# V weights in five pieces from ScalarE's queue, x blocks first in SyncE's queue, and a newly found order of the whole program

## The chip, the core and the metric

The kernel runs on one core of one Trainium2 chip. The metric is the device time of one execution in microseconds (us). Before the change it is 1747.95 us, the median of three runs (1744.44 to 1748.0).

## What is computed

Four layers one after the other over a sequence of 2048 rows of 512: memory-augmented attention A, a gated feed-forward block B, then A and B again with the same weights. Cut to what matters:

```python
def _A_ref(x, mem0, Wq, Wk, Wv, Wo, seg_len):      # H = 32 heads of 128, M = 8, seg_len = 32
    mem = mem0
    for s in range(S // seg_len):                  # 64 segments, one after the other
        h = concatenate([mem, x[:, s*seg_len:(s+1)*seg_len]], axis=1)      # 8 + 32 rows
        q, k, v = h @ Wq, h @ Wk, h @ Wv           # each 512 -> 32 heads x 128
        p = softmax(where(mask, q @ k.T * scale, -1e9))
        o = (p @ v) @ Wo
        mem = o[:, :8]                             # carried to the next segment
        outs.append(o[:, 8:])
def _B_ref(x, w_gate, w_up, w_down):
    return (sigmoid(x @ w_gate) * (x @ w_up)) @ w_down
x = x + _A_ref(layernorm(x), ...); x = x + _B_ref(layernorm(x), ...)       # twice
```

The carried memory makes the 64 segments of one attention layer a chain.

## The kernel before, in words

Both attention layers run interleaved: step t handles segment t of the first and segment t - 6 of the second (`emit_step`). A feed-forward block follows every four steps (`ffn`, 128 rows at a time, its weights streamed again each time from HBM by POOL's DMA queue). The weights of q, k, v and o (4 MB each) lie in SBUF for the whole run.

The stretch that this document is mostly about is the **boot**, up to the end of step 0:

- **Loads.** `load_weights` (L359) issues the weights from SyncE (SP): V in eight pieces of four heads (0.5 MB each, L370 to L374), each from the third on behind a wait for an earlier piece (`after`, L373, realised at L1233), with the x blocks that the boot needs put between them two at a time (L377). Then q and k in pieces of 3, 6 and 7 heads (384, 896 and 768 columns) and Wo in pieces of three heads. All DMAs of SP take one of eight semaphores in turn, so a DMA also waits until the DMA eight places before it has landed.
- **V in advance.** For most rows of the first layer V does not depend on the memory. `v_group` normalises an x block on VectorE (L582 to L586), transposes it on TensorE (L595), copies it to `xvf` on ScalarE or VectorE (L1228, L1230), and `v_pass` multiplies it with `wv_sb` (L635): eight groups of four matmuls of 512 columns per 128 rows, each group with its own 512 columns (four heads) of V. The results go through SBUF to a scratch tensor in DRAM (`scr`) and from there to `vsb`. Rows that do not fill a tile go through narrower strips of 64 columns (L673) and 32 columns (L762).
- **Step 0.** q and k (L868), scores (L904), softmax, transposed probabilities (L950), times V (L976), times Wo (L995). The first q and k matmuls can start as soon as their pieces of weights and the transposed x block 0 are there.
- **Fillers.** Where the plan sees TensorE without work for more than a quarter of a microsecond, it puts matmuls on a tile of zeros, `hot` (L1214), there to keep the clock up. At the start of the program this is a run of 23.

What comes when is not decided by the order of the Python lines. Each operation becomes a task of a planner (`Planner`). `SEQUENCE`, a packed string, holds the place of every task in one global order and, for tasks that two engines can do, the engine. `replay` walks this order with the planner's constants (durations, DMA rates, latencies), hands out buffers and computes where fillers go and what POOL's large weight loads are paced by. Each engine then runs its tasks in that order, and the waits between engines are derived from the data.

Of the kernel before, what the change touches and what calls it, by code (L numbers as in the profile page):

```python
# [1293 lines left out]
```

## Time and profile before

| | |
|---|---|
| median of three runs | 1747.95 us (1744.44, 1747.95, 1748.0) |
| span of the profiled execution, first to last instruction | 1747.1 us |
| TensorE (PE) busy | 1733.4 us, 99% |
| VectorE (DVE) busy | 1248.4 us, 71% |
| ScalarE (ACT) busy | 1128.5 us, 65% |
| GpSimd (POOL) busy | 859.0 us, 49% |
| moved by DMA | 273.41 MB, 156 GB/s over the span |
| granted TensorE clock | 1.000 |

Only the span of the profiled execution is known, not a time of its own; it lies between the lowest and the highest of the three runs. PE's busy time counts a matmul from its start to a modelled end, so that back-to-back matmuls leave no idle time; PEld is the loading of weights into the array, beside it. SP has no busy time: it only issues DMAs, and its rows (SPq) show when an issue began and how long it took. A releaser after an arrow is who ended the idle time before an instruction.

### The profile page before, as it was taken

The page shows a single profiled execution, that of the slowest core. Times are in us where ns is not written, and L with a number is a line of the kernel's source. Part 1 is how long each engine was busy: PE and PEld are TensorE (multiplying, and loading weights), DVE is VectorE, ACT ScalarE, POOL GpSimd, SP SyncE. Part 2 cuts the span into 40 slices and gives each one's busy share as a digit, 9 for nine tenths or more (in the row PEclk, how much of TensorE's full clock was granted, in tenths as well). Part 3 has the DMA queues.
Part 4 walks back from the last instruction along what each step waited for, and adds up shares of the span by engine and source line. Part 5 has one row for each costly group of instructions (what it writes and reads, how often), then busy time and mean ns, then how long its engine had stood idle before and what let it go on. Part 6 is the DMA issues. An engine that isn't in the chain of part 4 may idle for free.

```text
span 1747.1 us, 91842 instructions
## 1 busy us (share of the span) xinstructions
PE 1733.4 (99%) x39162; PEld 1491.8 (85%) x39162; DVE 1248.4 (71%) x4208; ACT 1128.5 (65%) x3119; POOL 859.0 (49%) x1367
## 2 busy tenths in 40 slices
PE   9999999999999999999999999999999999999998
PEld 4688789889898988989888888989888888988886
DVE  5677777677767776786777767776777776767676
ACT  3576777566666766666666666666665666666564
POOL 5624345635544554445445554544455364454543
PEclk9999999999999999999999999999999999999999
DMA  8935355645645555545555464545455464554644
GB/s 285 320 100 155 109 151 161 195 113 153 174 130 163 156 159 143 165 125 164 152 148 158 136 184 128 166 138 153 132 174 166 139 174 128 144 156 131 178 120 134
DMA packets 145583, 273.41 MB, mean 156 GB/s; under 512 B 39686, under 2 KB 86018, under 8 KB 145174
## 3 DMA queue, kind: packets, MB, share of 16 engines
q0 software_dynamic: 72944, 198.79, 39.8%
q1 hardware_dynamic: 72230, 68.75, 13.3%
q8 instruction: 307, 5.03, 1.2%
q14 instruction: 102, 0.84, 0.2%
HBM read 221.78 MB, written 27.07 MB: 142 GB/s over the span
## 4 chain that ended last, share of the span: by engine, by line
PE 94%; DMA 3%; DVE 1%; SPq 1%; issue 1%; POOL 0%; ACT 0%; POOLq 0%; ACTq 0%
PE bank L868 34%; PE bank L995 17%; PE bank L1097 12%; PE bank L762 8%; PE bank L635 6%; PE bank L1120 6%; PE bank L904 4%; PE bank L976 4%; PE bank L950 2%; PE bank L595 1%; PE bank L1214 1%; DMA wk_sb<-in_A_Wk_dram 1%; DMA wo_sb<-in_A_Wo_dram 0%; PE bank L1065 0%; DMA scr<-wu 0%
## 5 line engine op out<-in xcount | busy, mean ns | idle before, releaser
L868 PE MATMUL bank<-hT,wq_sb 128*128 128x80 bf16 (+3 forms) x8960 | 616.4, 198 | 1.0 <-DVE hT L1008 0.3
L868 PE MATMUL bank<-hT,wk_sb 128*128 128x80 bf16 (+3 forms) x8960 | 616.3, 198 | 0.8 <-DMA wk_sb<-in_A_Wk_dram 0.6
L1228 ACT CAST qku<-bank 128x480 bf16<-128x480 f32 (+4 forms) x770 | 384.7, 508 | 223.7 <-PE bank L868 194.6
L868 PEld LDWEIGHTS <-wq_sb 128*128 128x128 bf16 x8960 | 454.2, 99 | 32.1 <-issue 15.1
L868 PEld LDWEIGHTS <-wk_sb 128*128 128x128 bf16 x8960 | 446.9, 99 | 1.1 <-DMA wk_sb<-in_A_Wk_dram 0.7
L995 PE MATMUL bank<-otsb,wo_sb 128*128 128x80 bf16 (+1 forms) x8960 | 360.2, 198 | 2.2 <-DMA wo_sb<-in_A_Wo_dram 1.3
L918 DVE TENSOR_TENSOR st<-bank,cst 40x240 f32<-40x240 f32 (+3 forms) x768 | 280.5, 368 | 113.2 <-PE bank L904 97.5
L995 PEld LDWEIGHTS <-wo_sb 128*128 128x128 bf16 x8960 | 336.6, 99 | 15.5 <-DMA wo_sb<-in_A_Wo_dram 2.0
L1228 ACT CAST otsb<-bank 128x480 bf16<-128x480 f32 (+3 forms) x420 | 200.2, 483 | 83.4 <-PE bank L976 52.8
L1090 POOL DMA_DIRECT2D wu<-in_B_w_up_dram x217 | 166.5, 768 | 170.0 <-PE bank L950 36.4
L1114 POOL DMA_DIRECT2D wd<-in_B_w_down_dram x217 | 156.9, 723 | 182.0 <-PE bank L1120 39.6
L1224 POOL DMA_DIRECT2D vsb<-sst x351 | 178.2, 512 | 129.6 <-ACT sst L1228 64.7
L1089 POOL DMA_DIRECT2D wg<-in_B_w_gate_dram x217 | 166.4, 767 | 138.1 <-PE bank L1097 56.7
L928 ACT ACTIVATE st<-st 80x240 f32<-80x240 f32 (+3 forms) x420 | 159.2, 381 | 58.0 <-DVE st L925 54.8
L1097 PE MATMUL bank<-xnT,wg 128*128 128x128 bf16 (+2 forms) x1784 | 171.5, 218 | 0.0
L1097 PE MATMUL bank<-xnT,wu 128*128 128x128 bf16 (+2 forms) x1784 | 171.1, 218 | 0.0
L930 DVE TENSOR_REDUCE small<-st 80x6 f32<-80x240 f32 (+3 forms) x420 | 151.5, 363 | 23.4 <-ACT st L928 20.2
L1220 ACT ACTIVATE ptsb<-bank,small 120x160 bf16<-120x160 bf16 (+3 forms) x430 | 156.6, 386 | 17.2 <-PE bank L950 10.7
L904 PE MATMUL bank<-qku 128*128 128x80 bf16 (+1 forms) x2240 | 162.7, 197 | 1.0 <-issue 0.9
L925 DVE TENSOR_TENSOR st<-st,small 80x240 f32<-80x240 f32 (+3 forms) x420 | 155.0, 370 | 5.7
L939 DVE TENSOR_TENSOR pb<-st,small 80x240 bf16<-80x240 f32 (+3 forms) x420 | 154.1, 370 | 5.7
L923 DVE TENSOR_REDUCE small<-st 80x6 f32<-80x240 f32 (+3 forms) x420 | 152.5, 364 | 6.2
(108 smaller groups left out, 2554.1 us busy)
## 6 DMA issues: line engine op xcount, KB each, us to landing
wg<-in_B_w_gate_dram POOLq DMA_DIRECT2D x220, 256.0 KB, 4.2
wu<-in_B_w_up_dram POOLq DMA_DIRECT2D x220, 256.0 KB, 4.2
wd<-in_B_w_down_dram POOLq DMA_DIRECT2D x220, 256.0 KB, 3.9
vsb<-scr SPq DMA_DIRECT2D x137, 66.0 KB
scr<-vst SPq DMA_DIRECT2D x90, 96.0 KB
vsb<-scr POOLq DMA_DIRECT2D x93, 66.0 KB, 3.4
vsb<-sst SPq DMA_DIRECT2D x179, 32.0 KB
vsb<-sst POOLq DMA_DIRECT2D x169, 32.0 KB, 2.8
```

What stands on the lines that cost most here:

```text
L868: nc.tensor.matmul(o_ap, lhsT=W[:, c, h * P:(h + 1) * P], rhs=mv(c), start=(c == 0), stop=(c == DC - 1))
L904: nc.tensor.matmul(s_all(SB)[:, w0 + i, :], lhsT=fview(qku[:, i, 0, 0:1], [(1, P)]), rhs=qku[:, i, 1, 0:ncol], start=True, stop=True)
L918: pl.add("DVE", dve_ns(n, True), lambda gsz=gsz, hs=hs, st=st, SB=SB, pj_=pj_, npj_=npj_, mk=mk, idx=idx: nc.vector.tensor_tensor(out=st[p ...
L928: pl.add("ACT", act_ns(n), lambda hs=hs, st=st: nc.scalar.activation(out=st[pr, hs], in_=st[pr, hs], func=ACTF.Exp, scale=self.scale), r=s ...
L995: nc.tensor.matmul(WB[:, c * ncol:(c + 1) * ncol], lhsT=self.wo[:, h, c * P:(c + 1) * P], rhs=otsb[:, hl, 0:ncol], start=(h == 0 and c == ...
L1089: pl.add("POOL", 760, lambda wg=wg, fs=fs: nc.gpsimd.dma_start(out=wg[:], in_=self.wgv[:, :, fs]), r=[("wo", self.H - 1)], w=[gk] + bt, la ...
L1090: pl.add("POOL", 760, lambda wu=wu, fs=fs: nc.gpsimd.dma_start(out=wu[:], in_=self.wuv[:, :, fs]), r=[("wo", self.H - 1)], w=[uk] + bt, la ...
L1097: nc.tensor.matmul(gu[:, 2 * i + k, 0:n], lhsT=W[:, c, i * P:(i + 1) * P], rhs=xnT[:, c, rw], start=(c == 0), stop=(c == DC - 1))
L1114: pl.add("POOL", 760, lambda wd=wd, ip=ip: nc.gpsimd.dma_start(out=wd[:], in_=self.wdv[:, 2 * ip:2 * ip + 2, :]), w=[dk] + (["boot"] if se ...
L1220: nc.scalar.activation(out=dst, in_=src, func=ACTF.Copy, scale=by)
L1224: {"SP": nc.sync, "POOL": nc.gpsimd}[tk.on].dma_start(out=got[1], in_=got[2])
L1228: nc.scalar.copy(out=dst, in_=src)
```

## The change

V's weights come in five pieces (two of 4 heads, three of 8 heads) instead of eight. A piece may be issued by SP or by ACT; in the new order all five are on ACT. The waits of one piece for another (`after`) are gone. The x blocks are put between the pieces three at a time in the list of tasks, and in the new order they lead SP's queue. In the planner, `replay` now keeps a queue of transfers each for SP, ACT and POOL, with new constants, counts ACT's table load, and lets the semaphores' turn of eight cover ACT's DMAs too. `SEQUENCE` is replaced: the order of the whole program, on all engines, is another one.

Cut to the parts that the text speaks of:

```diff
-    BUS, BUS0, SLOW, BIG, ROOM, TAIL = 345.0, 290.0, 18000.0, 300000, 1.0, 1200.0
-    LEAD = {"SP": 1000.0, "POOL": 1800.0}
-    FIRST = {"PE": 0.0, "ACT": 2040.0, "DVE": 980.0, "POOL": 3500.0, "SP": 750.0}
+    BUS, BUS0, SLOW, BIG, ROOM, TAIL = 335.0, 304.0, 20400.0, 300000, 1.0, 1850.0
+    TAILP, CP, STEAL, FIX = 1000.0, 142.0, 0.4, 12400.0
+    LEAD = {"SP": 600.0, "ACT": 600.0, "POOL": 2800.0}
+    FIRST = {"PE": 0.0, "ACT": 800.0, "DVE": 980.0, "POOL": 3500.0, "SP": 750.0}
+    TABLE = 1240.0
...
-        bus = wbus = 0.0
+        bus, wbus = {"SP": 0.0, "ACT": 0.0, "POOL": 0.0}, 0.0
...
+            if (e == "SP" or e == "ACT" and tk.nb) and len(lanes) >= 8:
+                t = max(t, lanes[-8])
...
+            if e == "ACT" and not tk.nb and not table:
+                table, t = True, max(t, free[e] + self.TABLE)
...
-        def ld(dst, src, nb, keys, after=()):
-            return pl.add("SP", 480, lambda: nc.sync.dma_start(out=dst, in_=src), r=after, w=keys, boost=self.boot(), lat=1750.0, nb=nb)
+        def ld(dst, src, nb, keys, after=(), engs=("SP",)):
+            return pl.add(engs, {e: 480 for e in engs}, lambda: ("dma", dst, src), r=after, w=keys, boost=self.boot(), lat=1750.0, nb=nb)
 
         xb = list(self.boot_x)[1:]
-        for h0, n in ((0, 4), (4, 4), (8, 4), (12, 4), (16, 4), (20, 4), (24, 4), (28, 4)):
+        for h0, n in ((0, 4), (4, 4), (8, 8), (16, 8), (24, 8)):
             cs = slice(h0 * P, (h0 + n) * P)
-            tk = ld(self.wv[:, :, cs], wv_v[:, :, cs], P * self.DC * n * P * 2, [("wv", h) for h in range(h0, h0 + n)], [("wv", h0 - 8)] if h0 > 4 else [])
-            if h0 > 4:
-                tk.after = pl.writer[("wv", h0 - 8)]
+            ld(self.wv[:, :, cs], wv_v[:, :, cs], P * self.DC * n * P * 2, [("wv", h) for h in range(h0, h0 + n)], (), ("SP", "ACT"))
             if h0 == 0:
                 continue
-            for b in xb[:2]:
+            for b in xb[:3]:
                 self.load_x(b, *self.boot_x[b])
-            xb = xb[2:]
+            xb = xb[3:]
...
-                    {"SP": nc.sync, "POOL": nc.gpsimd}[tk.on].dma_start(out=got[1], in_=got[2])
+                    {"SP": nc.sync, "ACT": nc.scalar, "POOL": nc.gpsimd}[tk.on].dma_start(out=got[1], in_=got[2])
```

What the built programs' orders say of the boot, as instructions and without times:

- ACT's list begins: V heads 8 to 15 (1 MB); V heads 0 to 3, which waits for the semaphore of heads 8 to 15; V heads 4 to 7, which waits for that of the fourth x block; the table load; the copy into `xvf` that the first V group needs; V heads 16 to 23, waiting for the semaphore of a later x block; two copies; V heads 24 to 31, waiting for that of a small piece of Wo. Of the four later pieces each waits for a semaphore because it is the ninth or a later DMA in the turn of eight.
- SP's list begins with seven x blocks without a wait, then four more x blocks (three of the boot and block 1), each waiting for an earlier one, then the memory rows, a piece of Wo, the mask, and the q and k pieces.
- The first V group works on heads 8 to 11 (before: heads 0 to 3). The run of fillers at the start has 18 matmuls (17 of 512 columns and one of 384) instead of 23 (22 and one).
- Before the first q and k matmuls stand 22 V groups (before: 28), and the 64-column strips come after them, no longer ahead. Before the first matmul of step 1 there are 48 V groups and all of step 0 in both orders. The group of fillers between step 0 and step 1 is gone; two groups of 1280 columns each stand within step 0. Behind step 1's begin both orders hold nearly as many filler columns (11648 and 11776).

More of the change, by code (lines that the diff above doesn't have):

```diff
@@ new lines @@
+Ozvhl{wNq&Z&=^Qwg0xG0I{`(WWfk0i;>jDnf>k!)w-*;tC^*Gr{Nk-Jk3$19f=%hL5-5fXHxHV5&H#3q2kh^pB^)AueZdi~_o69owJ$zVTJgO=>FasOQ5XsL#N`p=tGvU9~86fs#sNiVT?EtZ^@z`=SB&cop<(@?_Nju`{73CCD%5
+45RNy#NQ^S1j!ah7e{Umg@8Ai{46i4eazo%+8kO=u@+igZ@AsDcjPyYaObY9wkN&!nvWWO<YyBtm<PbHfVa<`aLaZ5mbnBmj4M6XK6CI(eHooE-ti5DKN+nhN~1bY6H27+TC0k!-)_PlnAqQA*VN3Byce$s3D@L4UfTBb4Mu_jkq$u
+g6F`(yU~z9s>guSnT%Oo#|p^4&`ihU^E430QcM_4NY9Du#-&VbKQbK2I{9qCMM&zENc3cr>+$4{+Z)GGH&fHZ22j)i^v8&;BGI!r;RUCLWXZ6S#6sj-k(SvCK%v95!z}pS&N9rJLF>cW)Eob?8ZO=DaDIJ}j<MkcEH=ba!DupjdOqI
@@ L145 @@
+rFjzBBlr?Z9Fc4IlI3C_GnUQ~smjd)a(}7yYldAT4Lk?xnFl5xhT?fZ%jdy0`L!NpBzWwbunVnHb86tuRRE6$U|^kUsoMZ$do;LsKxm&hc%!Yc4f61*>bkP@7*LINHX#__gef@=EF%ebpeykkosL1+n_ms$=gU&A!qBmKAIpaE@aPB
+(Dr=NE+Nh;^K|l#q@kdQCkxNw-`@ZIBg%((*-Lm2U2C8SiUS++y4XLW3000
 """
@@ L276, in replay @@
         reads = {}
-        bus = wbus = 0.0
+        bus, wbus = {"SP": 0.0, "ACT": 0.0, "POOL": 0.0}, 0.0
         lanes, pes = [], []
+        table = False
         def ready(d, tk, gap):
@@ L320, in replay @@
             if tk.nb:
-                bus = max(bus, t + self.LEAD[e])
-                bus += tk.nb / (self.BUS0 if bus < self.SLOW else self.BUS)
-                tk.done = max(bus + self.TAIL, end + tk.lat + tk.slow * min(max(wbus - t, 0.0), self.BACK))
+                a = t + self.LEAD[e]
+                w = (tk.nb + self.FIX) / (self.BUS0 if t < self.SLOW else self.BUS)
+                late = min(max(wbus - t, 0.0), self.BACK)
+                if e == "POOL":
+                    busy = [q for q in ("SP", "ACT") if bus[q] > a]
+                    for q in busy:
+                        bus[q] += self.STEAL * w / len(busy)
+                    if busy:
+                        w = (tk.nb + self.FIX) / self.CP
+                else:
+                    q = "ACT" if e == "SP" else "SP"
+                    d = min(w, max(bus[q] - a, 0.0))
+                    bus[q] += d
+                    w += d
+                bus[e] = max(bus[e], a) + w
+                landed = bus[e] + (self.TAILP if e == "POOL" else self.TAIL)
+                tk.done = max(landed, end + tk.lat + tk.slow * late)
                 if e == "POOL" and tk.nb >= self.BIG:
                     wbus = max(wbus, t + self.LEAD[e]) + tk.nb / self.BUS
-            if e == "SP":
+            if e == "SP" or e == "ACT" and tk.nb:
                 lanes.append(tk.done)
-                if len(lanes) >= 8:
-                    free[e] = max(end, lanes[-8])
         self.span = max(free.values())
@@ L360, in waits @@
         for d in [T[i] for i in list(tk.deps) + tk.prev]:
-            k = d.on if d.on != "SP" else ("SP", d.tick)
+            k = d.on if d.on != "SP" and not (d.on == "ACT" and d.nb) else (d.on, "dma", d.tick)
             if d.tick > seen.get(k, 0):
```

175 lines of the change are left out of this document (83 added, 92 removed).

## The prediction

> **What bounds the kernel now.** I read the page first, for which engine is full. It shows the span, the busy times and the shares of the chain that ended last:
>
> ```profile
> span 1747.1 us, 91842 instructions
> PE 1733.4 (99%) x39162; PEld 1491.8 (85%) x39162; DVE 1248.4 (71%) x4208; ACT 1128.5 (65%) x3119; POOL 859.0 (49%) x1367
> PE 94%; DMA 3%; DVE 1%; SPq 1%; issue 1%; POOL 0%; ACT 0%; POOLq 0%; ACTq 0%
> ```
>
> PE is busy for all but 13.7 us, and neither program does less matrix work. So all there is to win is idle time of PE, and fillers that stand where real work could. Then the table of stretches, to see where the idle time lies. A row has the stretch, its length, the busy time of PE, PEld, DVE, ACT and POOL, the granted clock, the mean busy share of the DMA engines and GB/s:
>
> ```profile
> 0.00:2.30 2.30, 1.24 (x3) 0.43 (x4) 0.12 (x2) 1.28 (x1) 1.41 (x13) 1.00 0.10 21
> 2.30:4.50 2.20, 2.20 (x7) 0.78 (x6) 0.00 (x0) 0.00 (x0) 0.40 (x3) 1.00 1.04 318
> 4.50:9.00 4.50, 4.50 (x21) 1.99 (x20) 3.02 (x8) 0.00 (x0) 1.85 (x4) 1.00 0.91 294
> 9.00:20.00 11.00, 11.00 (x63) 5.18 (x59) 7.65 (x21) 4.37 (x8) 5.95 (x14) 1.00 0.83 263
> 20.00:40.00 20.00, 17.64 (x119) 8.04 (x118) 11.26 (x28) 7.72 (x19) 12.75 (x25) 1.00 0.93 311
> 40.00:80.00 40.00, 37.91 (x627) 23.62 (x625) 23.43 (x75) 21.21 (x63) 23.88 (x46) 1.00 1.00 341
> 80.00:300.00 220.00, 219.15 (x5641) 185.88 (x5637) 161.86 (x577) 161.61 (x531) 95.73 (x156) 1.00 0.49 137
> 300.00:1600.00 1300.00, 1298.90 (x28799) 1145.63 (x28799) 937.65 (x3140) 846.55 (x2222) 648.59 (x1006) 1.00 0.54 152
> 1600.00:1747.10 147.10, 140.85 (x3909) 120.21 (x3901) 103.43 (x359) 85.73 (x278) 68.43 (x102) 1.00 0.50 143
> ```
>
> PE's idle time is 2.36 us from 20 to 40, 2.09 from 40 to 80, 0.85 + 1.10 from 80 to 1600 and 6.25 at the end. Who ended that of the boot is in the list of waits of PE up to 80 us (total us, times, longest):
>
> ```profile
> PE bank L635 <- DMA wv_sb<-in_A_Wv_dram: 2.4, 2, 1.9
> PE bank L995 <- DMA wo_sb<-in_A_Wo_dram: 1.3, 3, 0.6
> PE bank L868 <- DMA wk_sb<-in_A_Wk_dram: 0.6, 1, 0.6
> PE bank L868 <- DMA wq_sb<-in_A_Wq_dram: 0.2, 1, 0.2
> ```
>
> All of it is weights that land late: 2.4 us for V, 2.1 us for the other three. From 40 to 80 us the DMA share is 1.00; ahead of 40 it is not. Last the order in time, for PE, where it starts and where step 0 begins and ends:
>
> ```profile
> 1.06 7.77 PE L1214 MATMUL bank<-hot 128*128 128x512 bf16 x23 [1.06 <-DVE cst L484]
> 8.67 0.39 PE L595 MATMUL bank<-cst,xn 128*128 128x128 bf16 x4
> 8.89 0.54 PE L1214 MATMUL bank<-hot 128*128 128x512 bf16 x2
> 9.27 0.39 PE L595 MATMUL bank<-cst,xn 128*128 128x128 bf16 x4
> 9.50 0.76 PE L1214 MATMUL bank<-hot 128*128 128x512 bf16 x3
> 10.23 1.04 PE L635 MATMUL bank<-wv_sb,xvf 128*128 128x512 bf16 x4
> ...
> 20.79 2.76 PE L635 MATMUL bank<-wv_sb,xvf 128*128 128x512 bf16 x12 [0.45 <-DMA wv_sb<-in_A_Wv_dram]
> ...
> 25.69 1.04 PE L635 MATMUL bank<-wv_sb,xvf 128*128 128x512 bf16 x4 [1.91 <-DMA wv_sb<-in_A_Wv_dram]
> ...
> 40.83 3.64 PE L673 MATMUL bank<-wv_sb,xvl 128*64 128x512 bf16 x32
> 44.41 0.27 PE L868 MATMUL bank<-hT,wq_sb 128*128 128x54 bf16 x4
> ...
> 79.26 0.48 PE L1214 MATMUL bank<-hot 128*128 128x512 bf16 x2
> 79.70 0.23 PE L868 MATMUL bank<-hT,wq_sb 128*128 128x54 bf16 x3
> ```
>
> Real work begins at 10.23 us and step 1 at 79.70. Between them lie the 4.45 us of idle time and 0.44 us of fillers; the rest, 64.6 us, is the same matmuls in both orders.
>
> **Part 1: when the first V group starts.** Today it starts 10.23 us in. Three things must be there: the transposed x (PE's own list), the copy into `xvf` on ACT, and the first V piece.
>
> PE's list loses five fillers of 512. One more of them made 0.22 us of difference between the runs of 0.54 and 0.76 us above, so by PE's list alone the group could start at 10.23 - 1.1 = 9.13. The x blocks come no later than that needs:
>
> ```profile
> 0.81 0.46 SPq L511 DMA_DIRECT2D wv_sb<-in_A_Wv_dram  x1
> 1.33 0.96 SPq L724 DMA_DIRECT2D xs<-in_A_x_dram  x2
> ...
> 4.51 0.38 SPq L511 DMA_DIRECT2D wv_sb<-in_A_Wv_dram  x1
> ```
> ```profile
> 4.86 0.69 DVE L582 BATCH_NORM_STATS2 small<-xs 128x6 f32<-128x512 bf16 x1 [3.85 <-DMA xs<-in_A_x_dram]
> ...
> 7.74 0.72 DVE L586 TENSOR_SCALAR xn<-xs,small 128x512 bf16<-128x512 bf16 x1 [0.45 <-POOL small L585]
> ```
>
> Today the first x block is the second DMA, lands at 4.86, and the second block is normalised at 8.46. First in the queue it is issued 0.5 us sooner and has no 0.5 MB ahead of it, so 8.0 at the latest.
>
> ACT is another matter. Its list now starts with a 1 MB piece, then two pieces of which the first waits for that one to land, then the table load, and only then the copy:
>
> ```profile
> 0.81 1.28 ACT L1228 ACT_TABLE_LOAD   x1 [0.81 <-PEq L1275]
> 9.70 0.48 ACT L1228 COPY xvf<-bank 128x384 bf16<-128x384 bf16 x1 [7.61 <-PE bank L595]
> ```
>
> So from the landing of the 1 MB it takes two issues (ACT issues none today; SP's take 0.38 to 0.48 us, I take 0.46), 1.28 and 0.48: 2.7 us. When does it land? Today's first 0.5 MB, issued at 0.81, has landed by 4.51, when the piece that waits for it is issued: 3.70 us. Another 0.5 MB at the 318 GB/s of that stretch makes 6.2 us if nothing else moves. Seven x blocks (0.92 MB) are issued beside it; all of them first would add 2.9, 9.1 us. How two hardware queues share the engines no row shows, since only SP's exists today. I take the middle of the bounds, 7.6, so the copy ends and the group starts at 10.3. **Part 1: +0.1 us, bounds -1.1 (9.13) and +1.6 (9.1 + 2.7 = 11.8).**
>
> The Trainium skill ("DMA: Bandwidth & Descriptors", "Queues, rings and completion order") says that each DMA engine takes turns between the queues, a packet at a time. The rows of V pieces would be twice as long as those of x, so that by this rule half as many bytes of x (0.52 MB) would go beside the 1 MB, and the estimate from the rule is a landing at 6.2 + 1.6 = 7.8 and part 1 at +0.3. That changes nothing that I forecast; no run here shows it yet.
>
> **Part 2: the waits for V, 2.36 us.** The last V piece lands late because its issue stands behind waits:
>
> ```profile
> SPq L511 <- DMA wv_sb<-in_A_Wv_dram: 8.8, 5, 3.2
> ```
> ```profile
> 18.17 7.47 DMA wv_sb<-in_A_Wv_dram
> 69.99 8.54 DMA wo_sb<-in_A_Wo_dram
> ```
>
> The first view is SP's own waits up to 80 us, the second two links of the chain of waits: the last piece is issued at 18.17 and lands at 25.65. In the new order it is ACT's fourth issue after the first. Ahead of it on ACT stand the copy into `xvf`, the 16-to-23 piece (waiting for a late x block), and two copies, the first of the group's result. Two groups at 0.9 us (12 matmuls in 2.76 us above), 0.6 for the copy and the issues put it at about 10.3 + 3.2 = 13.5, and with the slowest latency of the old one it has landed at 21.0. PE asks for it after twelve groups and four sets of transposes (0.22 us each, 8.67 to 8.89): 10.3 + 10.8 + 0.9 = 22.0. It fits, with a microsecond to spare. Behind each waiting issue ACT's evictions of V stand, but ACT has only 4.37 us of work in the 11 us of that row. **Part 2: -2.2 us, bounds -2.36 and 0.**
>
> **Part 3: the waits for q, k and o, 2.1 us, and an earlier demand.** Without the V waits, six V groups (5.3 us) and the 64-column strips (3.6) PE reaches the first q and k matmuls 11 us sooner, at some 33 us instead of 44.4, and asks for the 896-column pieces, which come next, some 10 us later, at 43.5. By then 11.6 MB stand ahead on SP's and ACT's queues (V 4.2, x 1.7, q and k 5.2, the rest 0.5), and some 2 MB on POOL's. The stretches above moved 4.96 MB by 20 us and 11.2 by 40; at 341 GB/s 13.6 MB are reached at 47.1. At today's pace PE would stand 3.6 us there. But today the engines are idle for 1.4 us from 20 to 40 and for 2.2 between 2.3 and 20, behind the waits that go. If all of that is used, nothing is lost there, and the last piece of Wo, 8.54 us under way in the chain, lands earlier by as much, so that the 2.1 us go. Between 0 and 3.6 I take half, 1.8 lost, as no row is nearer to one end, and 2.1 won. **Part 3: -0.3 us, bounds -2.1 and +3.6.**
>
> **Part 4: fillers.** The new order has two groups of 1280 columns in step 0: 2.5 matmuls at 0.22, 0.55 us each, 1.1 us if the work behind them is ready, nothing if it is late anyway. The 0.44 us ahead of step 1 goes. **+0.6 us, bounds -0.44 and +0.66.**
>
> **Part 5: the rest of the program.** The order changes everywhere, on every engine. From 80 to 1600 us PE has 1.95 us of idle time in all, so there is little to win; the last 147 us have 6.25, much of it the drain of the last rows. Fillers are as many as before. With its new constants the planner lets POOL's weight loads go earlier; the DMA share of 0.49 to 0.54 covers that. I take 0, bounds -2 and +2.
>
> **The sum**: 0.1 - 2.2 - 0.3 + 0.6 = -1.8 us. Against the profiled execution 1745.3; that execution's span is 0.85 under the median of the runs, so against the median 1747.95 - 1.8, about **1746.1 us**.
>
> **Rivals.**
>
> *The boot stays bound by DMA (1747.5).* From 40 to 80 us the engines are full. If the last piece of Wo still lands where it does, everything won before is waited for there, and only fractions remain: 1747.95 - 0.4. For it speaks the share of 1.00; against it the idle 3.6 us ahead of 40. The Trainium skill says (same page, "Issuing engines are not separate DMA queues") that transfers issued from several engines run on the same DMA engines and that only the time of issuing is saved; by this rule a second queue gains nothing where the share is 1.00, but what goes here is waiting.
>
> *More is won (1742).* The order holds against late transfers, so PE is fed all along: parts 2, 3 and 4 at their good ends, -2.36 - 2.1 - 0.44, and a microsecond of part 5: -5.9. For it speaks that every idle microsecond of the boot is a late DMA; against it that the whole trace has no more than that.
>
> *Slower (1752): PE asks for q and k before they are there.* It reaches the 896-column pieces at 43.5, and they land at 47.1 as worked out above; ACT's waits cost the start +1.6 and half of the V waits stay: 1.6 - 1.2 + 3.6 + 0.6 - 0.5 (Wo) = +4.1. It decides from about 3.6 us on: with the other parts as forecast the sum is zero when PE stands that long ahead of 50 us, instead of the 1.8 I took.
>
> That the pieces have "no waits for each other" is only half true in the built order: the second waits for the first by its semaphore. That is priced in part 1.
>
> **How the numbers follow.** This kernel's measurement can tell about 0.2%, 3.5 us, from no change. The forecast (1744 to 1748) 38%, of which 10 lie below 1744.45; more won 26%, faster; bound by DMA 18%, same; slower 18%, of which 2 stay within 0.2%. So faster 36%, same 48%, slower 16%. The ends of all bounds together lie 8 us off on either side; 8 in 10 lie between 1741 and 1752, from the second rival to the third. The forecast's own range is 1744 to 1748.
>
> **What would show it.** Part 1: the first V group's start, and whether ACT's copy or a DMA ended the idle time before it. Part 2: no row of L648 (the new number of L635) behind a V transfer. Part 3: PE's idle time ahead of q and k matmuls between 33 and 50 us, and ahead of Wo; step 1 should begin at about 78 instead of 79.70. Part 5: idle time from 80 us on within 2 us of today's. The forecast is wrong if ACT's start comes after 11 us, or if step 1 begins where it does now.

## The result, and the profile after

The changed kernel takes 1757.18 us, the median of six runs (1752.61 to 1760.69); the kernel before takes 1747.68 beside it, also of six (1743.06 to 1749.5). The ratio is 1.0059, with a 95% interval from 1.0043 to 1.0074: the change costs about 10.3 us. Forecast was 1746.1, with 8 chances in 10 between 1741 and 1752. The profiled execution took 1757.5 us, 1.7 more than its span.

The head of the profile after:

```profile
span 1755.8 us, 91762 instructions
PE 1736.2 (99%) x39161; PEld 1492.3 (85%) x39161; DVE 1258.1 (72%) x4172; ACT 1144.8 (65%) x3155; POOL 867.7 (49%) x1393
```

The span grew by 8.7 us. PE's busy time grew by 2.8 of them, without more matrix work; 5.9 are idle time. The table of stretches says where (stretch, length, busy time of PE, PEld, DVE, ACT and POOL, granted clock, DMA share, GB/s):

```profile
9.00:20.00 11.00, 9.44 (x54) 4.20 (x54) 9.26 (x27) 5.42 (x14) 5.81 (x13) 1.00 1.01 332
20.00:40.00 20.00, 19.94 (x181) 9.84 (x179) 15.20 (x42) 8.30 (x20) 16.79 (x33) 1.00 0.85 286
40.00:80.00 40.00, 36.84 (x559) 22.84 (x555) 22.71 (x67) 18.14 (x52) 29.30 (x55) 0.96 1.03 358
80.00:300.00 220.00, 215.73 (x5515) 181.56 (x5514) 158.02 (x555) 156.07 (x515) 90.01 (x148) 1.00 0.46 131
300.00:1600.00 1300.00, 1298.78 (x28773) 1143.98 (x28770) 946.21 (x3118) 865.96 (x2268) 652.23 (x1020) 1.00 0.53 152
1600.00:1755.80 155.80, 148.63 (x4077) 127.35 (x4073) 103.86 (x359) 89.90 (x287) 69.07 (x105) 0.99 0.46 136
```

PE's idle time (length less busy time) is now 1.6 us from 9 to 20 (before: none), 0.1 from 20 to 40 (2.4), 3.2 from 40 to 80 (2.1), 4.3 from 80 to 300 (0.85) and 7.2 from 1600 on (6.25). So part of what is gone between 20 and 40 stands ahead of 20 now. Two rows have a granted clock below 1, which no row of before has.

The waits of PE up to 80 us (total, times, longest):

```profile
PE bank L989 <- DMA vsb<-scr: 1.9, 1, 1.9
PE bank L881 <- DMA wk_sb<-in_A_Wk_dram: 1.2, 1, 1.2
PE bank L608 <- DVE xn L599: 1.1, 1, 1.1
...
PE bank L648 <- DMA wv_sb<-in_A_Wv_dram: 1.0, 1, 1.0
```

Wo is gone from this list, V is still in it, and the read-back of V from the scratch tensor (`vsb` from `scr`) is new. PE's list in time, for where they stand:

```profile
10.14 1.90 PE L648 MATMUL bank<-wv_sb,xvf 128*128 128x512 bf16 x8
...
19.67 3.63 PE L648 MATMUL bank<-wv_sb,xvf 128*128 128x512 bf16 x16 [0.98 <-DMA wv_sb<-in_A_Wv_dram]
...
47.67 0.28 PE L881 MATMUL bank<-hT,wk_sb 128*128 128x54 bf16 x4 [1.22 <-DMA wk_sb<-in_A_Wk_dram]
...
76.44 0.21 PE L989 MATMUL bank<-ptsb,vsb 80*128 80x80 bf16 x1 [1.94 <-DMA vsb<-scr]
...
80.88 0.26 PE L881 MATMUL bank<-hT,wq_sb 128*128 128x54 bf16 x4
```

The first V group starts at 10.14 (before: 10.23), step 1 at 80.88 (79.70). ScalarE's list shows why V is still late:

```profile
0.80 7.11 ACTq L1237 DMA_DIRECT2D wv_sb<-in_A_Wv_dram  x3
...
13.12 0.37 ACTq L1237 DMA_DIRECT2D wv_sb<-in_A_Wv_dram  x1
13.54 0.59 ACT L1241 CAST wd<-bank 128x512 bf16<-128x512 f32 x1 [3.45 <-DMA xa<-in_A_x_dram]
13.59 0.47 ACTq L1237 DMA_DIRECT2D wv_sb<-in_A_Wv_dram  x1
```

Heads 16 to 23 are issued at 13.12, since ACT was idle for 3.45 us, nearly all of it for the turn of a semaphore that an x block held; PE wants them at 18.7 and gets them at 19.67.

Last the clock, in stretches of 3.41 us around the two places where it fell (columns as above):

```profile
73.58:77.00 3.42, 1.48 (x28) 0.95 (x26) 1.15 (x5) 0.98 (x3) 2.68 (x7) 1.00 1.05 342
77.00:80.41 3.41, 3.41 (x85) 2.92 (x81) 1.02 (x4) 0.92 (x3) 2.84 (x6) 0.50 0.71 214
...
1647.13:1650.54 3.41, 1.76 (x71) 1.66 (x68) 0.00 (x0) 0.88 (x3) 0.34 (x1) 1.00 0.68 225
1650.54:1653.95 3.41, 3.41 (x39) 1.28 (x39) 2.80 (x8) 1.35 (x3) 0.00 (x0) 0.50 0.04 13
```

PE was idle for 1.94 and 1.65 us, and for the next 3.41 us ran at half speed, which loses 1.7 us each time. Together 3.4 us, which covers the 2.8 us of busy time.

### The profile page after: what moved, and what is told of

It is laid out like the page before. It is cut to its first block, busy times and chain, and to the rows that moved or that the text cites. A ratio compares the mean times of both kernels' runs of the same rounds, so it can differ in the third digit from the quotient of the medians.

```text
span 1755.8 us, 91762 instructions
## 1 busy us (share of the span) xinstructions
PE 1736.2 (99%) x39161; PEld 1492.3 (85%) x39161; DVE 1258.1 (72%) x4172; ACT 1144.8 (65%) x3155; POOL 867.7 (49%) x1393
## 4 chain that ended last, share of the span: by engine, by line
PE 93%; DMA 3%; DVE 1%; issue 1%; ACT 1%; POOL 1%; SPq 0%; ACTq 0%; DVEq 0%; POOLq 0%
PE bank L881 34%; PE bank L1008 17%; PE bank L1110 11%; PE bank L775 7%; PE bank L648 7%; PE bank L1133 5%; PE bank L917 4%; PE bank L989 4%; PE bank L963 2%; PE bank L608 1%; DMA wv_sb<-in_A_Wv_dram 1%; DMA wk_sb<-in_A_Wk_dram 0%; PE bank L1078 0%; DMA scr<-wg 0%; DMA kx<-xq 0%
## 5 line engine op out<-in xcount | busy, mean ns | idle before, releaser
L1241 ACT CAST qku<-bank 128x480 bf16<-128x480 f32 (+2 forms) x770 | 384.0, 507 | 212.3 <-PE bank L881 182.8
L1008 PE MATMUL bank<-otsb,wo_sb 128*128 128x80 bf16 (+1 forms) x8960 | 356.5, 198 | 1.2 <-ACT st L941 0.5
L1237 POOL DMA_DIRECT2D vsb<-sst x336 | 169.8, 510 | 198.1 <-ACT sst L1241 63.5
L1237 POOL DMA_DIRECT2D vsb<-scr x210 | 110.9, 530 | 141.5 <-PE bank L989 55.2
L1233 ACT ACTIVATE ptsb<-bank,small 80x160 bf16<-80x160 bf16 (+3 forms) x458 | 165.9, 385 | 18.4 <-PE bank L963 13.7
```

Of the source, the lines that this page charges most:

```text
L1008: nc.tensor.matmul(WB[:, c * ncol:(c + 1) * ncol], lhsT=self.wo[:, h, c * P:(c + 1) * P], rhs=otsb[:, hl, 0:ncol], start=(h == 0 and c == ...
L1233: nc.scalar.activation(out=dst, in_=src, func=ACTF.Copy, scale=by)
L1237: {"SP": nc.sync, "ACT": nc.scalar, "POOL": nc.gpsimd}[tk.on].dma_start(out=got[1], in_=got[2])
L1241: nc.scalar.copy(out=dst, in_=src)
```

## The experiments

The theories that the expectations name:

- **B**: the whole loss is made in the boot. **R**: the boot loses a part, and the newly found order of the rest the larger part.
- **L**: V is late because of where its pieces are issued. **K**: what the boot wins on V it loses on k, whose pieces are issued late.
- **C**: idle time of PE costs twice, by the clock. **F**: waits whose releaser is called "issue" are PE's loading of its own instructions.

"At equal work" in them is the difference between the times at which two executions have begun the same amount of PE's work, counted by its weight loads with the columns that follow each. Line numbers differ by a few between kernels. In some of the traces some 200 of 39,161 matmul records are missing, so idle time is compared by the lists of waits. Every ratio is to runs of the kernel before on the same chip.

### Which part of the order costs what: four splices

Each keeps the changed kernel's code and constants, and replaces the packed order:

```diff
-SEQUENCE = the new order
+SEQUENCE = the first K tasks of the new order, then all other tasks as the old order has them
```

K is 640 (step 2 begins), 1660, 2180 and 12920. The changed code and the new constants of the planner are in all four; what they cost by themselves no run splits off.

**newboot_oldrest.** 

> The new order up to the beginning of step 2, from there on the tasks in the old order, with the new planner's constants. Theory B (the boot loses: late x, late k, late read-back of V, half clock): as slow as the changed kernel, about 1756 us. Theory R (the boot ends only 1.2 us behind, and the new order of the rest loses the other 7 to 8): about 1747.7 + 1.2 = 1749 us.

**newto197_oldrest.** 

> The new order up to about 197 us, the old one from there on. Theory R with its loss between 120 and 200 us (at equal work the changed kernel is 0.8 us behind at 120 us and 4.6 behind at 200): 1747.7 + 4.6 = 1752 us. If what counts lies after 200 us: about 1749. Theory B: about 1756.

**newto260_oldrest.** 

> The new order up to about 260 us, the old one from there on. Theory R says that the new order loses 1.6 us more between 200 and 250 us (4.6 behind at 200, 6.3 at 250 at equal work, in the changed kernel) and nothing from 250 to 1600: 1752.4 (spliced at 197 us) + 1.6 = 1754 us. If the loss lies all in the boot and up to 197: 1752.4; if it lies ahead of 260 altogether: as the changed kernel, 1757.

**newto1620_oldend.** 

> The new order up to about 1620 us, the old one for the last 130 us. Theory F (TensorE's instruction loading stalls it for 2.1 to 4.5 us after 1600 in the four executions of the new order, for 0.4 to 2.7 in those of the old): 2.5 to 3.5 us less than the changed kernel, about 1754 us. Rival (the end costs both orders the same): 1757.

| new order up to | median, us | ratio to before (95%) | that is |
|---|---|---|---|
| step 2 | 1750.33 | 1.0019 (1.0009 to 1.0029) | +3.3 us |
| 197 us | 1752.43 | 1.0030 (1.0018 to 1.0041) | +5.2 |
| 260 us | 1756.28 | 1.0038 (1.0024 to 1.0053) | +6.6 |
| 1620 us | 1754.99 | 1.0034 (1.0024 to 1.0044) | +5.9 |
| the end (the changed kernel) | 1757.18 | 1.0059 (1.0043 to 1.0074) | +10.3 |

B falls: with the old order from step 2 on, two thirds of the loss are gone. R is right in kind, though the boot's part is larger than the 1.2 us that it gave. The boot costs some 3.3 us, the stretch up to 260 another 3.3, the 1360 us after that nothing, and the last 130 some 4.4. Neighbouring rows overlap, so a single step is known to about 2 us; the first and the last row don't overlap.

The waits of PE from 100 to 300 us agree. First the changed kernel, then newboot_oldrest (its longest), then newto260_oldrest:

```profile
PE bank L775 <- issue: 1.3, 2, 1.0
PE bank L989 <- ACT ptsb L1233: 1.1, 1, 1.1
PE bank L1133 <- DMA wd<-in_B_w_down_dram: 0.7, 1, 0.7
```
```profile
PE bank L987 <- DMA vsb<-scr: 0.2, 1, 0.2
```
```profile
PE bank L879 <- issue: 1.6, 2, 1.2
PE bank L1131 <- DMA wd<-in_B_w_down_dram: 1.4, 1, 1.4
PE bank L773 <- issue: 1.3, 1, 1.3
```

In all seven traces in which the new order holds there, PE waits 0.7 to 1.6 us for weights of the feed-forward block (`wd`), and in no trace of the old order. "Issue" is mostly longer with the new order (0.2 to 2.9 us in sum from 80 to 300, against 0 to 1.9). The wait for ScalarE's copy (`ptsb`) stands in three of the seven traces only, so it isn't a cost of the order in every execution. From 1600 on "issue" is the largest wait: 3.2 us (2.0 + 0.7 + 0.5) in the changed kernel's trace, 2.5 in that of before and 0.7 (0.4 + 0.3) in that of newto1620_oldend. Single traces don't decide this; the part on the prediction counts all of them.

### Where V is issued

**v_on_sp.** One queue, in the order in which PE asks (the numbers are tasks: x blocks and V pieces in turn):

```diff
             fill = self.pl.warm(order)
+            lead = [self.pl.tasks[i] for i in [23, 22, 24, 21, 19, 18, 20, 221, 28, 26, 32]]
+            for tk in lead:
+                tk.on = "SP"
+            order = lead + [tk for tk in order if tk not in lead]
```

> The changed kernel, but SyncE issues the five pieces of V and the x blocks in one queue, in the order in which TensorE asks for them; order, fillers and pacing of everything else stay. Theory L (the third and fourth pieces of V come late because their issue stands on ScalarE behind a copy and a semaphore's turn, at 13.1 us, and their neighbours on the other queue take turns with them): waits for V under 0.5 us instead of 1.0 to 3.7, about 3 us less than the changed kernel, 1754 us. Rival (the engines are full, the bytes come no sooner from another queue): waits for V of 1 to 3 us as before, 1757 us.

Measured: 1755.76 us, 1.0041 (1.0027 to 1.0054), some 3 us better by the ratio, though the intervals overlap. The longest waits of PE up to 80 us:

```profile
PE bank L648 <- ACT wd L1245: 2.2, 2, 1.1
PE bank L881 <- DMA wk_sb<-in_A_Wk_dram: 1.8, 1, 1.8
```

No wait for V's transfers is left, and the first V group starts at 9.12. L is right about V. But evictions (`wd` is the staging buffer here) now hold PE for 2.2 us, and k for 1.8.

**v_on_sp_oldrest.** The same edit on newboot_oldrest. 

> As the one before, and from step 2 on the old order. Theories L and R together (the boot loses on V's landing, the rest on its order): 1750.3 less 3, about 1747 us, level with the kernel before or a little ahead. If L is wrong: about 1750 us.

Measured: 1750.03 us, 1.0010 (1.0001 to 1.0019). The gain of 3 us didn't come as forecast; in its trace V waits for nothing, and k for more:

```profile
PE bank L879 <- DMA wk_sb<-in_A_Wk_dram: 3.6, 2, 2.1
```

After the second of these waits the clock was at half from 50.97 on, for 3.41 us.

**qk_early.** v_on_sp_oldrest, and

```diff
+            early = [self.pl.tasks[i] for i in (35, 47, 50, 49)]
+            order = [tk for tk in order if tk not in early]
+            k = order.index(self.pl.tasks[48]) + 1
+            order[k:k] = early
```

> As v_on_sp_oldrest, and four pieces of q and k (one of 384, three of 896 columns, 3.1 MB) are issued ahead of six writes of V to the scratch tensor, instead of behind them: in that run SyncE stood from 24.1 to 29.6 us on the first of these writes, the engines were 0.36 to 0.66 busy from 18 to 25, and TensorE waited 3.6 us for k at 45 to 50. Theory K (what the boot gains on V it loses again on k, since the pieces of k are issued late): the waits for k fall from 3.6 to under 1 us, no half clock at 51 us, 1750.0 less 3, about 1747. Rival (the engines are full from 25 us on, the wait moves on to Wo or to the read-back of V): 1749 to 1750.

Measured: 1753.39 us, 1.0030 (1.0019 to 1.0042): slower. The waits for k are gone, and the pieces of q that come after them are later:

```profile
PE bank L879 <- DMA wq_sb<-in_A_Wq_dram: 3.7, 1, 3.7
```

K was half the matter. The pieces were late, but what is put ahead pushes back what is asked for next. The DMA engines are full from 25 to 42 us, but not in the 8 us after that: SyncE stands for one of the writes to the scratch tensor that now come behind the pieces. Its wait, and a stretch of that time (columns as above):

```profile
SPq L1243 <- DMA scr<-sst: 6.4, 1, 6.4
```
```profile
44.00:46.00 2.00, 2.00 (x58) 1.42 (x51) 0.26 (x1) 0.58 (x1) 1.02 (x2) 1.00 0.12 29
```

The wait ends at 43.8, and the next pieces of q are issued at 47.7 only (45.2 in v_on_sp_oldrest), though the engines were 0.12 to 0.61 busy from 42 to 50. The rival is right that the wait moves on; it moved to q, not to Wo or the read-back, and the time is above the rival's.

**hand_move.** The old order with only the queue and the waits of V changed:

```diff
-        def ld(dst, src, nb, keys, after=()):
-            return pl.add("SP", 480, lambda: nc.sync.dma_start(out=dst, in_=src), ...
+        def ld(dst, src, nb, keys, after=(), eng=nc.sync):
+            return pl.add("SP", 480, lambda: eng.dma_start(out=dst, in_=src), ...
...
-            tk = ld(self.wv[:, :, cs], ..., [("wv", h0 - 8)] if h0 > 4 else [])
-            if h0 > 4:
-                tk.after = pl.writer[("wv", h0 - 8)]
+            tk = ld(self.wv[:, :, cs], ..., [("wv", h0 - 8)] if h0 > 4 else [], nc.scalar)
```

> The old order and the old eight pieces, but ScalarE issues the pieces of V, and they don't wait for each other; everything else stays, planner and fillers too. If that part of the change is good by itself: the 2.4 us of waits for V go, 1745.5 us, no worse start. If the V pieces on a queue of their own hold up the x blocks: first V group 1 to 3 us later than 10.23, time 1748 to 1750 us.

Measured: 1754.87 us, 1.0041 (1.0026 to 1.0055). The x blocks come sooner, and V comes later, for a reason that I had not named. ScalarE's list:

```profile
9.79 0.48 ACT L1226 COPY xvf<-bank 128x384 bf16<-128x384 bf16 x1 [7.22 <-PE bank L593]
9.80 0.37 ACTq L511 DMA_DIRECT2D wv_sb<-in_A_Wv_dram  x1
...
14.90 0.59 ACT L1226 CAST wd<-bank 128x512 bf16<-128x512 f32 x1 [2.91 <-PE bank L633]
14.90 8.19 ACTq L511 DMA_DIRECT2D wv_sb<-in_A_Wv_dram  x5
```

The issue of the second piece stands behind a copy that waits for PE until 9.79, those of the next five behind an eviction that waits for PE until 14.9, and PE waits for V: 6.1 us, and the clock is at half from 13.56 to 27.2. ScalarE works through one list, so a DMA that it issues waits for its compute.

**no_waits.** The other half of the hand-made change alone:

```diff
-            if h0 > 4:
-                tk.after = pl.writer[("wv", h0 - 8)]
```

> The kernel before with nothing changed but the waits of one piece of V for another taken out; same queue, same order. If these waits made V late: the 2.4 us go, about 1745.5 us. If the turn of eight semaphores holds the pieces back as long, or the engines are full: no difference, 1747.3 us. If the pieces then go ahead of small transfers that are asked for sooner: slower, 1749.

Measured: 1747.31 us, 1.0001 (0.9991 to 1.0012): no difference. Its trace has no wait for V and 2.0 us for q and k, and is short (span 1743.2); in the median of 11 runs nothing is left of that.

**no_waits_qk.** no_waits with the same four lines as qk_early, for tasks 50, 52 and 53 behind 51. 

> The old order without the waits of one piece of V for another, and three pieces of q and k of 896 columns issued ahead of the writes to the scratch tensor that stood before them. Theory K: the 2.0 us of waits for q and k at 53 and 59 us go, 1747.3 less 1.5, about 1746. Rival: they move on to Wo, 1747 to 1748.

Measured: 1752.21 us, 1.0022 (1.0009 to 1.0035). Waits for q and k are gone, Wo isn't late either, and a third party is:

```profile
PE bank L593 <- ACT wu L1230: 4.5, 1, 4.5
```
```profile
46.56 0.58 ACT L1230 CAST wu<-bank 128x512 bf16<-128x512 f32 x1 [5.84 <-DMA scr<-wu]
```

The writes to the scratch tensor that were put behind free the staging buffers into which V's results are evicted; without a free one the eviction waits, its bank stays taken, and PE stands 4.5 us. The rival was right that the wait moves on, wrong about where and about the price.

### The clock and the instructions

**fill_at_wait.** The changed kernel and

```diff
             fill = self.pl.warm(order)
+            tk = order[499]
+            fill[tk.idx] = (tk.acq[0], 32)
```

> The changed kernel with eight filler matmuls of 512 columns (1.7 us) ahead of the L989 that waits 1.94 us for the read-back of V in step 0; no work is added to the path, since PE waits there anyway. Theory C (the idle time makes the granted clock fall to one half for 3.41 us, 1.7 us lost): no half clock ahead of 100 us, 1.7 us less than the changed kernel, about 1755.5 us. Rival (the clock falls for another reason, or not in every execution): as the changed kernel, 1757.2, with a window of half clock near 77 us as before.

Measured: 1758.26 us, 1.0067 (1.0053 to 1.0081): nothing won. At that place the clock stayed at 1; but in this execution V came 2.0 us late and k 2.3, and the clock fell behind those:

```profile
48.99:52.40 3.41, 1.14 (x23) 0.89 (x25) 0.00 (x0) 0.99 (x5) 2.04 (x4) 1.00 1.06 401
52.40:55.81 3.41, 3.23 (x14) 1.27 (x14) 1.26 (x4) 0.33 (x2) 2.22 (x5) 0.50 1.06 393
```

C's mechanism is seen again, its price not by this run. Where the boot's waits are long enough to make the clock fall differs from one execution to the next.

**shift.** The first run of fillers in more pieces:

```diff
-                    m = min(n, 4)
+                    m = min(n, 1 if tk is first else 4)
```

> The changed kernel with its first run of fillers cut into 71 matmuls of 128 columns instead of 18 of up to 512: the same columns, but 106 instructions more ahead of everything. Theory F (waits whose releaser is named issue are TensorE's own instruction loading: in both kernels they end at every 256th instruction of its list, a remainder of 194): those at 171.9 us (L775, 1.0 us) and 1648.8 us (L917, 1.65 us) are gone, and others stand at other instructions, with the same remainder; time as the changed kernel, 1755 to 1759. Rival (the order makes them): the same instructions wait again.

Measured: 1759.57 us, 1.0061 (1.0047 to 1.0075), as the changed kernel. At 168 to 180 and 1640 to 1660 us there is no wait called "issue" any more; others have come, this one the longest at the end:

```profile
PE bank L989 <- issue: 1.3, 1, 1.3
```

All nine of them over 0.25 us stand at the same remainder by 256 as in the other traces (see the end). So the order doesn't make these waits at a given instruction; F is right. What it costs to have them is about the same at another place.

No version beats both kernels. The two nearest to the kernel before are no_waits (1.0001) and v_on_sp_oldrest (1.0010).

## Why the prediction was wrong

- **Part 1** (+0.1 us): the start is where I put it, 10.14 for 10.3, but not for my reasons, so the number is luck: the 1 MB landed at 6.44 where I took 7.6, and ACT then stood for an x block, so that its table load began at 7.95 only. The clause that failed is that the x blocks come no later than needed. The second block's normalisation begins at 8.65 and takes 0.46, where I had 8.0 at the latest, and PE stood 1.1 us for it:

```profile
6.79 0.69 DVE L595 BATCH_NORM_STATS2 small<-xs 128x6 f32<-128x512 bf16 x1 [2.11 <-DMA xs<-in_A_x_dram]
...
8.65 0.46 DVE L599 TENSOR_SCALAR xn<-xs,small 128x512 bf16<-128x512 bf16 x1 [0.44 <-POOL small L598]
```

- **Part 2** (-2.2): failed. Three links of the chain of waits of the changed kernel (start, length) serve this part and the next:

```profile
13.59 9.95 DMA wv_sb<-in_A_Wv_dram
...
61.75 7.03 DMA scr<-wg
...
71.71 4.68 DMA vsb<-scr
```

  I timed the issue of the last piece well (13.5; it was 13.59), but gave a piece of 1 MB the latency of one of 0.5 MB, 7.47 us; it takes 9.95 and lands at 23.54. And I did not time the piece before it, which PE wants first. Over seven executions of this boot (the changed kernel, four splices, fill_at_wait, shift) the waits for V are 1.0, 3.7, 3.1, 3.9, 1.1, 2.0 and 1.8 us, a mean of 2.4, as much as in the one trace of the kernel before. The part is 0. That the 2.36 us were there to win was read from that one trace, too: no_waits has none of them in its trace and is no faster in the median.
- **Part 3** (-0.3): q and k were right in kind, and in size by the middle of two far bounds. The waits for k in those executions are 1.2, 1.8, 1.7, 1.5, 1.3, 2.3 and 2.0, a mean of 1.7 where I took 1.8, and Wo's waits are gone as forecast. What failed is the clause "so that the 2.1 us go": the read-back of V takes Wo's place, with 1.9 us in the trace of the changed kernel (0.4 to 1.9 in the seven, a mean of 1.3), since V is evicted, written and read back while the same engines bring k and Wo (7.03 us from 61.75 for the write, 4.68 from 71.71 for the read). No step of mine priced that path.
- **Not in the sum**: idle time that makes the clock fall costs 1.7 us more. The kernel before stood 1.91 us at 23.6 and its clock held, so I had no row for it; of the seven executions above, the clock fell at least once in all but two ahead of 100 us, six times in all. As an estimate, the forecast's -1.8, the 2.2 us of part 2 that didn't come, 1.3 for the read-back and 1.5 for the clock (6 x 1.7 / 7) make +3.2 us, near the 3.3 that newboot_oldrest measured for the boot.
- **Part 4** (+0.6): as forecast, two runs of fillers of 0.54 us each.
- **Part 5** (0, -2 to +2): the largest failure, some 7 of the 10.3 us by the splices. The working was that the old order has 1.95 us of idle time there, "so little to win". That bounds what can be won. It says nothing on what can be lost, and an order that nobody has run on the chip has its own late waits: 3.3 us up to 260 and 4.4 at the end. Of the first, `wd` is shown, and "issue" in most traces. Of the second, PE's loading of instructions is nearly half, by an estimate: stretches of over 0.2 us idle after 1600 that end 1.0 to 1.9 us behind an instruction packet sum to 3.7, 2.3, 3.6 and 4.5 us in the four executions of the new end (after, fill_at_wait, v_on_sp, shift; mean 3.5) and 0.4 to 2.7 in ten of the old one (mean 1.4), 2.1 of the 4.4. Why the new end meets more of it stays open, and so does the rest of the 4.4.
- **The rivals**: the time came out past the slower one, 1752, whose mechanism does not decide. It needed 3.6 us of waiting ahead of 50 us, and there are 1.2 for k in the trace. The forecast's own sign of error, that step 1 begins no sooner than before, is what happened (80.88 after 79.70).

## What to carry to other kernels

Where a change replaces the whole order of a program, the idle time of the old order bounds the gain but not the loss: give the part that "only moves" a wide range to the bad side (here it lost some 7 us). A DMA issued by an engine that also computes waits behind its compute and for semaphores' turns; before you take a wait out, write down when each such issue can leave, and for every piece, not only for the last. Where the DMA engines are full, putting one transfer ahead puts the next one behind, and with it whatever the queue then waits for.

## What the runs showed of the hardware

- **The clock.** It falls to one half for 3.41 us, or for a whole number of such windows (13.65 us in hand_move, 6.83 in no_waits_qk), and all falls of one execution lie a whole number of 3.413 us apart (77.00 and 1650.54: 461 times). In such a window ahead of the fall PE was idle for 1.57 to 3.16 us (13 falls, in ten traces); windows with up to 1.95 us idle passed without one, such as that of before at 23.60 (1.91). The Trainium skill ("TensorE: Matmul & The Clock Gate", "HAM oscillation — how this bites in real kernels") gives as a rule that PE should not idle for more than some 3.4 us; the traces here differ: 1.57 us, in sum over one such window, were enough.
- **Instruction loading.** PE's longer waits for "issue" end 1.2 to 1.6 us after a packet of 16 KB of the instruction queue has ended. Counted over PE's matmuls, weight loads and sequencer rows, all seven of those over 0.25 us in the trace of the changed kernel (one of them put down to ScalarE there), and the five over 0.25 in that of before, stand at a remainder of 193 or 194 by 256. The page's row of that queue:

```profile
q8 instruction: 307, 5.03, 1.2%
```

  makes one packet per 256 of the 78,686 rows. The packet of 1647.99 started 2.6 us after PE had begun the block before, while POOL's weights took 79.2% of the engines' time (1646 to 1650), and PE was through the block at 1648.82:

```profile
1648.42 0.25 PE L881 MATMUL bank<-hT,wq_sb 128*128 128x40 bf16 x4
1648.52 0.25 PE L881 MATMUL bank<-hT,wk_sb 128*128 128x40 bf16 x4
1648.62 0.20 PE L917 MATMUL bank<-qku 128*128 128x40 bf16 x2
1650.47 0.40 PE L917 MATMUL bank<-qku 128*128 128x40 bf16 x7 [1.65 <-issue]
```

  In that stretch groups of four matmuls and their four weight loads follow each other in 0.10 us, so 256 instructions are through in 3.2 us. The Trainium skill ("Runtime: NRT & Kernel Launch", "Instruction fetch mechanics") has the block of 256 and says that its cost is mostly hidden; the trace agrees on the block and on "mostly": of some 307 crossings seven show more than 0.25 us. At these it is not hidden, 1.65 us at the worst.
- **Two hardware queues.** From 3 to 6 us the queue of ScalarE (q10, the 1 MB of V) and that of SyncE (q1, x blocks, issued as early) moved (packets, MB, share of 16 engines):

```profile
q10 hardware_dynamic: 494, 0.98, 85.0%
q1 hardware_dynamic: 200, 0.19, 17.8%
```

  Turns of one row each, which is how the prediction worked out the rule of the Trainium skill, would have given x half as many bytes as V; it got a fifth, and the second x block landed for its statistics to begin at 6.79, just after V's had landed at 6.44. The section that the prediction cites ("DMA: Bandwidth & Descriptors", "Queues, rings and completion order", of the Trainium skill) lets a packet hold several descriptors, so the trace speaks against the prediction's working, and is no test of the rule.
